# Ordering GpSimd's subtractions, the weight conversions and the activation in the last stage of a fused attention and mixture kernel

## The chip, the cores and the metric
The kernel runs on one core of one Trainium2 chip. The metric is the device time of one execution in microseconds. Before the change it is 782.74 us, the median of three runs (780.12 to 784.16).

## The reference, cut to what matters
The program is attention over 4 x 8 heads with pooled queries, a soft mixture of experts, and a feed-forward block in float32 whose weights come as 64-bit floats. The change touches the last part only:

```python
def _moe2_ref(x, w_in, w_out):          # x 2304 x 512, w_in 512 x 2048, w_out 2048 x 512
    h = x @ w_in
    beta = 1.0
    neg = h <= -beta
    pos = h >= beta
    g = np.where(pos, h, np.where(neg, 0.0, (h + beta) ** 2 / (4.0 * beta)))
    return (g @ w_out).astype(np.float32)
```

x itself is the product c @ slot_out of a 2304 x 32 matrix and a 32 x 512 matrix, so the kernel computes h as c @ (slot_out @ w_in).

## The kernel before, in words
All stages are written out in an order fixed by hand: each engine executes its instructions in the order of the program text, and waits only for data and for buffers. TensorE is first kept busy with attention (to some 450 us after the start), then with the mixture, and from about 535 us on with the last stage.

The last stage works on 36 blocks, SEQ: four quarters q of the 2048 inner columns, and in each nine groups of 256 rows. For block k:

- **h_unit(k)** (L955) lets TensorE multiply Mst (slot_out @ w_in of this quarter) by cT: four matmuls of 256 columns into two PSUM tiles of the pool hp, which has four buffers, so two units. A first clamp or relu goes into the tile cl: on ScalarE where k % 3 is 1 or 2 (L961), on VectorE otherwise (L963).
- **g_unit(k)** (L966) finishes the activation: one or two passes of ScalarE over 1024 columns (L969, L970, L972), then two additions of VectorE, r (L975), which read the PSUM tiles of h. After them the tiles are free for the unit two further on.
- **g_split(k)** (L981) cuts r into two float32r parts: ghi on ScalarE (L984) and glo = r - ghi on GpSimd (L985).
- **o_part(k, tt)** (L1022, matmuls at L1025): 12 output matmuls of 512 columns for each half tt of the rows, ghi by WHI, ghi by WLO, glo by WHI. **o_out** (L1033) adds the PSUM tile to PA in SBUF on VectorE (L1037); in the first quarter it copies, one half on ScalarE (L1041), one on VectorE (L1039). In the last quarter it also issues the store. The pool po of these PSUM tiles has four buffers and is shared with M and its copies.

Beside this the weights are turned from 64-bit to 32-bit floats: **cv_abs** (L185, L189) on ScalarE and the four steps of **cv_step** (L191; L196, L198, L201, L204) on VectorE, the last of which issues the load two pieces on, on SP's queue. Conversion n of 12 to 31 belongs to the block listed in CVB. A converted piece of w_out is split by **w_hi** (ScalarE, L898) and **w_lo** (L902; GpSimd for the quarters 1 to 3, VectorE for quarter 0). **m_mm(q)** (L926) multiplies slot_out by the converted w_in of quarter q and splits the result into Mhl; **m_rep(q)** (L935) spreads it by four matmuls (Mr) into Mst, half on ScalarE (L946), half on VectorE (L944). MB lists the block of m_mm; m_rep follows a block later.

What sets the order around the change is the loop over k: conversion of block k, then ahead(k + 4) (L1051), which runs unit_step(k + 3): g_split(k + 1), g_unit(k + 2), h_unit(k + 3). Then the outputs:

```python
            conv(k, 0, 4)
            ahead(k + AHEAD + 1)
            if sp:
                w_lo(*sp)
            if k < len(SEQ) - 1:
                o_part(k, 0, pos[0])
                ...
                o_out(k, 0, pos[0])
                o_part(k, 1, pos[1])
                o_out(k, 1, pos[1])
                conv_abs(k + 1)
```

Blocks 0 and 1 of the activation go through first_unit (L999) in smaller pieces, and block 0 is mixed by hand with units 2 and 3.

Of the kernel before, what the change touches and what calls it, by code (L numbers as in the profile page):

```python
# [48 lines left out]
def fused_kernel(ctx: ExitStack, tc: tile.TileContext, q, k, v, phi, w1, w2, w_in, w_out, out):  # L49
# [123 lines left out]
    cv = {}  # L173
# [479 lines left out]
    with tc.manual_schedule():  # L653
# [239 lines left out]
            nc.sync.dma_start(out=Wst[:, x:x + 4, :], in_=cv_dr[:, x:x + 4, :])  # L893
        soT = wsp.tile([128, 4, NS], F32, name="soT")
        Mhl = wsp.tile([128, 2, 128], F32R, name="Mhl")

        def w_hi(q, j):
            nc.scalar.activation(out=WHI[q % 2][:, j, :], in_=Wst[:, j, :], func=AF.Copy)  # L898

        def w_lo(q, j):  # L900
            eng = nc.gpsimd if q else nc.vector
            eng.tensor_tensor(out=WLO[q % 2][:, j, :], in0=Wst[:, j, :], in1=WHI[q % 2][:, j, :].bitcast(F32), op=ALU.subtract)  # L902

        for e in range(E_):
            s2o(e, 1)
# [47 lines left out]
            return ps  # L953

        def h_unit(k):  # L955
            cl = t_p.tile([128, 4, TB], F32, tag="cl", name=f"cl{k}")
# [9 lines left out]
        def g_unit(k):  # L966
            cl, ps = hq[k]
            if k % 3:
                nc.scalar.activation(out=cl, in_=cl, func=AF.Relu, scale=-1.0, bias=two)  # L969
                nc.scalar.activation(out=cl, in_=cl, func=AF.Square, scale=-0.5, bias=ones)  # L970
            else:
                nc.scalar.activation(out=cl, in_=cl, func=AF.Square, scale=-0.5, bias=half)  # L972
            r = hq[k] = t_p.tile([128, 4, TB], F32, tag="r", name=f"r{k}")
            for a in (0, 2):
                nc.vector.scalar_tensor_tensor(out=r[:, a:a + 2], in0=ps[a // 2], scalar=-1.0, in1=cl[:, a:a + 2], op0=ALU.max, op1=ALU.add)  # L975

        def g_tiles(k):
# [1 line left out]
            glo[k] = g_p.tile([128, 4, TB], F32R, tag="glo", name=f"glo{k}")  # L979

        def g_split(k):  # L981
            r = hq.pop(k)
# [4 lines left out]
        def unit_step(i):  # L987
            if 3 <= i - 2 < len(SEQ):
                g_split(i - 2)
            if 4 <= i - 1 < len(SEQ):  # L990
                g_unit(i - 1)
            if i < len(SEQ):
                h_unit(i)


        FU = [(0, 0, 1), (0, 1, 2), (0, 2, 3), (0, 3, 4), (1, 0, 2), (1, 2, 4)]
        fu = {}
# [48 lines left out]
        def o_tiles(k):  # L1046
            return [po_tile(f"po{k}_{tt}") for tt in range(2)]

        nu = 4

        def ahead(n):  # L1051
            nonlocal nu
            while nu < min(n, len(SEQ) + 2):
                unit_step(nu)
                nu += 1

        cvb = dict(zip(CVB, range(12, 32)))

        def conv(k, i0, i1):
            if k in cvb:  # L1060
                for i in range(i0, i1):
                    cv_step(cvb[k], i)

        def conv_abs(k):
            if k in cvb:
                cv_abs(cvb[k])

        def split_of(k):
            if k in cvb and cvb[k] % 8 >= 4:
                return cvb[k] // 8, cvb[k] % 8 - 4  # L1070

        c_xpose(1)
        m_mm(0)
# [14 lines left out]
        for k in range(len(SEQ)):  # L1088
            if k:
                pos = o_tiles(k)  # L1090
            if k == 0:
                o_first(0, pos, 0)
                first_unit(5)
                o_first(0, pos, 1)
                first_unit(6)
                h_unit(2)
                g_unit(2)
                o_first(0, pos, 2)
                h_unit(3)
# [5 lines left out]
                conv_abs(1)  # L1105
                continue
            sp = split_of(k - 1)
            if sp:
                w_hi(*sp)
            conv(k, 0, 4)  # L1110
            ahead(k + AHEAD + 1)
            if sp:
                w_lo(*sp)
# [51 lines left out]
```

## Time and profile before

| what | before |
|---|---|
| median of three runs | 782.74 us |
| the profiled execution's own time | 780.04 us |
| its span, first to last instruction | 778.3 us |
[...]
| busy: TensorE, VectorE, ScalarE, GpSimd | 744.0, 618.3, 464.8, 125.1 us |
| instructions | 18103 |

The page shows one profiled execution. [...] The starts of matmuls tell the pace. VectorE is busy in 79% of the span, GpSimd almost only in the last stage. Rows below are named by their group.

### The profile page before, as it was taken

To read this page: it belongs to the slowest core of one execution; us is meant where nothing else is said; L and a number is where in the kernel's file an instruction comes from. 1 tells how busy PE (TensorE), PEld (TensorE's weight loads), DVE (VectorE), ACT (ScalarE), POOL (GpSimd) and SP (SyncE) were. 2 spreads that over 40 slices of the span, in tenths; PEclk is the share of its full clock that TensorE was granted. 3 is DMA by queue.
4 is the path that set the end of the run, shared out by engine and by line. 5 is a ranking of instruction groups with operands and counts; after the bars stand their busy time and mean duration, and the time that the engine had idled before them with its cause. 6 is when DMAs were issued, how large, how long until landed. Compare 5 with 4: busy or idle time off the path is not lost.

```text
span 778.3 us, 18103 instructions
## 1 busy us (share of the span) xinstructions
PE 744.0 (96%) x7422; PEld 544.6 (70%) x7422; DVE 618.3 (79%) x1000; ACT 464.8 (60%) x853; POOL 125.1 (16%) x86
## 2 busy tenths in 40 slices
PE   7789999999999999999999998999899999999998
PEld 6567777766777757777657765436677777778887
DVE  5788898988989969989969774525799998987443
ACT  4246667667567657667656665106876766567660
POOL 7200000000000000000000000002363445246441
PEclk8899999999999999999999999999999999999999
DMA  9697478758667838867938466992112211200122
GB/s 211 125 216 178 92 209 203 158 151 194 159 163 196 210 82 197 194 167 166 238 64 237 141 213 228 365 391 106 52 57 81 83 54 55 82 27 1 55 96 94
DMA packets 133603, 116.55 MB, mean 150 GB/s; under 512 B 80144, under 2 KB 98832, under 8 KB 133136
## 3 DMA queue, kind: packets, MB, share of 16 engines
q1 hardware_dynamic: 133520, 115.40, 54.9%
q8 instruction: 58, 0.95, 0.5%
q14 instruction: 25, 0.20, 0.1%
HBM read 81.85 MB, written 7.86 MB: 115 GB/s over the span
## 4 chain that ended last, share of the span: by engine, by line
PE 71%; DVE 18%; DMA 4%; ACT 3%; issue 3%; SPq 1%; DVEq 0%; ACTq 0%
PE st L366 17%; PE acc L396 16%; PE po L1025 13%; PE mx L300 9%; PE acc L389 3%; DVE r L975 3%; DVE Wst L201 2%; DVE Wst L198 2%; DVE Wst L196 2%; PE tx L434 2%; PE s2o L829 2%; DVE mp L312 2%; PE h L777 1%; DVE pa L1037 1%; PE tb L461 1%
## 5 line engine op out<-in xcount | busy, mean ns | idle before, releaser
L371 ACT ACTIVATE e<-st 128x576 f32<-128x576 f32 x288 | 187.1, 651 | 124.4 <-PE st L366 120.0
L312 DVE TENSOR_REDUCE mp<-mx 128x1 f32<-128x576 f32 x282 | 211.6, 754 | 42.8 <-PE mx L300 42.4
L396 PE MATMUL acc<-e,vf 128*64 128x288 f32 x1152 | 193.8, 408 | 0.0
L300 PE MATMUL mx<-K,q 128*64 128x288 f16 x1152 | 124.6, 297 | 10.6 <-DVE mp L312 3.9
L366 PE MATMUL st<-q,K 128*64 128x288 f16 x1152 | 122.3, 287 | 6.7 <-ACT e L371 4.8
L366 PE MATMUL st<-q,S 128*64 128x288 f16 x1152 | 122.2, 286 | 0.0
L379 DVE TENSOR_TENSOR es<-es,e 128x576 f32<-128x576 f32 x160 | 119.8, 750 | 0.0
L300 PEld LDWEIGHTS <-q 128*64 128x64 f16 x1152 | 66.5, 111 | 70.4 <-issue 24.8
L1025 PE MATMUL po<-whi,ghi 128*128 128x512 f32 x280 | 110.7, 395 | 0.0
L1025 PE MATMUL po<-wlo,ghi 128*128 128x512 f32 x280 | 110.0, 393 | 0.0
L1025 PE MATMUL po<-whi,glo 128*128 128x512 f32 x280 | 109.7, 392 | 0.0
L985 POOL TENSOR_TENSOR glo<-r,ghi 128x1024 fp32r<-128x1024 f32 x34 | 83.0, 2440 | 119.6 <-ACT ghi L984 119.5
L366 PEld LDWEIGHTS <-K 128*64 128x64 f16 x1152 | 68.5, 109 | 24.1 <-issue 14.6
L396 PEld LDWEIGHTS acc<-e,vf 128*64 128x64 f32 x1152 | 78.4, 137 | 5.5 <-ACT e L371 1.6
L754 POOL MEMSET xfer<- 128x1024 f32 x1 | 1.0, 957 | 471.0 <-PE pb L557 471.0
L366 PEld LDWEIGHTS <-S 128*64 128x64 f16 x1152 | 69.9, 110 | 3.0
L1037 DVE TENSOR_TENSOR pa<-po,pa 128x512 f32<-128x512 f32 (+1 forms) x54 | 35.8, 682 | 36.8 <-PE po L1025 36.4
L1025 PEld LDWEIGHTS po<-whi,glo 128*128 128x128 f32 x280 | 53.2, 190 | 11.4
L1025 PEld LDWEIGHTS po<-whi,ghi 128*128 128x128 f32 x280 | 53.5, 191 | 10.8 <-ACT cl L961 0.2
L1025 PEld LDWEIGHTS po<-wlo,ghi 128*128 128x128 f32 x280 | 53.5, 191 | 9.7
L984 ACT ACTIVATE ghi<-r 128x1024 fp32r<-128x1024 f32 x34 | 36.0, 1059 | 36.5 <-DVE r L975 36.5
L975 DVE SCALAR_TENSOR_TENSOR r<-h,cl 128x512 f32<-128x512 f32 x68 | 43.6, 683 | 12.1 <-ACT cl L970 10.6
(197 smaller groups left out, 873.5 us busy)
## 6 DMA issues: line engine op xcount, KB each, us to landing
w<-in_moe_w_dram SPq DMA_DIRECT2D x31, 1024.0 KB, 7.5
vf<-in_v_dram SPq DMA_DIRECT2D x16, 576.0 KB, 4.4
kf<-in_k_dram SPq DMA_DIRECT2D x30, 288.0 KB, 3.6
f<-in_moe_w_in_dram SPq DMA_DIRECT2D x16, 512.0 KB, 4.3
f<-in_moe_w_out_dram SPq DMA_DIRECT2D x16, 512.0 KB, 3.6
qf<-in_q_dram SPq DMA_DIRECT2D x30, 256.0 KB, 4.6
S<-K SPq DMA_DIRECT2D x16, 288.0 KB, 3.2
out_dram<-pa SPq DMA_DIRECT2D x17, 256.0 KB, 2.0
```

The source lines that it names most:

```text
L300: nc.tensor.matmul(ps[p0:p1, i, 0:HQ], lhsT=q1[P][:, t, p0:p1], rhs=kk[:, j * HQ:(j + 1) * HQ], start=True, stop=True)
L312: nc.vector.tensor_reduce(out=mp[P][:, t, a:a + 1], in_=ps[:, :, 0:HQ], op=ALU.max, axis=AX.XY)
L366: nc.tensor.matmul(ps[c0:c0 + 64, i, 0:HQ], lhsT=kk[:, ci, c0:c0 + 64], rhs=f[:, sl[i]], start=first, stop=not first)
L371: nc.scalar.activation(out=e, in_=ps[:, :, 0:HQ], func=AF.Exp, scale=ESC)
L379: nc.vector.tensor_tensor(out=Es[P, n, h][:, i0:i1], in0=a[:, i0:i1], in1=b[:, i0:i1], op=ALU.add)
L389: nc.tensor.matmul(acc[P, i][32 * j:32 * j + 32, HQ:HQ + c1 - c0], lhsT=ones.to_broadcast([128, 32]), rhs=src[:, j % 2, c0:c1], start=Fals ...
L396: nc.tensor.matmul(acc[P, i][h * 64:(h + 1) * 64, 0:HQ], lhsT=vt[P][:, h, c, :], rhs=E[P, c, h][:, i, :], start=(c == 0), stop=(c == NK - ...
L975: nc.vector.scalar_tensor_tensor(out=r[:, a:a + 2], in0=ps[a // 2], scalar=-1.0, in1=cl[:, a:a + 2], op0=ALU.max, op1=ALU.add)
L984: nc.scalar.activation(out=ghi[k], in_=r, func=AF.Copy)
L985: nc.gpsimd.tensor_tensor(out=glo[k], in0=r, in1=ghi[k].bitcast(F32), op=ALU.subtract)
L1025: nc.tensor.matmul(ps, lhsT=a, rhs=b, start=st_, stop=sp)
L1037: nc.vector.tensor_tensor(out=t, in0=po, in1=t, op=ALU.add)
```

## The change
In the last stage, from block 4 on, the order in a block becomes: conversion (or two low parts of w_out), g_unit(k + 3), the absolute value for the next block's conversion, a ScalarE copy of one column out of what the conversion or low part wrote last (junk), and g_split(k + 2). As ScalarE works in order, ghi and with it glo start only when VectorE has finished the conversion. h_unit(k + 4) stands between the two halves of the outputs. Blocks 1 to 3 have steps of their own that bring the activation one block further ahead, with no such copy. Every unit has one half of its first pass on ScalarE and one on VectorE, and 512-wide ScalarE passes. The low parts go to VectorE, two in a block, in blocks without a conversion (5, 6, 15, 16, 25, 26), with their high parts on ScalarE the block before; conversions are in blocks 1 to 4, 7 to 14 and 17 to 24. m_mm is one block later (3, 11, 21), m_rep in the same block after its second half.

```diff
-AHEAD = 3
-CVB = 1, 2, 3, 4, 5, 6, 7, 8, 9, 10, 11, 13, 14, 15, 17, 18, 19, 21, 22, 24
-MB = {1: 2, 2: 10, 3: 20}
+MB = {1: 3, 2: 11, 3: 21}
...
         def w_lo(q, j):
-            eng = nc.gpsimd if q else nc.vector
-            eng.tensor_tensor(out=WLO[q % 2][:, j, :], in0=Wst[:, j, :], in1=WHI[q % 2][:, j, :].bitcast(F32), op=ALU.subtract)
+            nc.vector.tensor_tensor(out=WLO[q % 2][:, j, :], in0=Wst[:, j, :], in1=WHI[q % 2][:, j, :].bitcast(F32), op=ALU.subtract)
...
-            ps = []
-            for a in (0, 2):
-                ps.append(h_mm(k, a, a + 2))
-                if k % 3:
-                    nc.scalar.activation(out=cl[:, a:a + 2], in_=ps[-1], func=AF.Relu, scale=-1.0, bias=ones)
-                else:
-                    nc.vector.tensor_scalar(out=cl[:, a:a + 2], in0=ps[-1], scalar1=-1.0, scalar2=1.0, op0=ALU.max, op1=ALU.min)
+            ps = [h_mm(k, a, a + 2) for a in (0, 2)]
+            nc.scalar.activation(out=cl[:, 0:2], in_=ps[0], func=AF.Relu, scale=-1.0, bias=ones)
+            nc.vector.tensor_scalar(out=cl[:, 2:4], in0=ps[1], scalar1=-1.0, scalar2=1.0, op0=ALU.max, op1=ALU.min)
...
-            if k % 3:
-                nc.scalar.activation(out=cl, in_=cl, func=AF.Relu, scale=-1.0, bias=two)
-                nc.scalar.activation(out=cl, in_=cl, func=AF.Square, scale=-0.5, bias=ones)
-            else:
-                nc.scalar.activation(out=cl, in_=cl, func=AF.Square, scale=-0.5, bias=half)
+            nc.scalar.activation(out=cl[:, 0:2], in_=cl[:, 0:2], func=AF.Relu, scale=-1.0, bias=two)
+            nc.scalar.activation(out=cl[:, 2:4], in_=cl[:, 2:4], func=AF.Square, scale=-0.5, bias=half)
+            nc.scalar.activation(out=cl[:, 0:2], in_=cl[:, 0:2], func=AF.Square, scale=-0.5, bias=ones)
...
-            for a in (0, 2):
+            for a in (2, 0):
                 nc.vector.scalar_tensor_tensor(out=r[:, a:a + 2], ...)
...
                 h_unit(2)
+                o_first(0, pos, 2)
                 g_unit(2)
-                o_first(0, pos, 2)
-                h_unit(3)
+                o_first(0, pos, 3)
                 g_split(2)
-                g_unit(3)
-                o_first(0, pos, 3)
...
+            steps = [(h_unit, 3), (g_unit, 3)], [(h_unit, 4)], [(g_split, 3)]
+            if k == 2:
+                steps = [(g_unit, 4), (g_split, 4)], [(h_unit, 5)], [(g_unit, 5)]
+            elif k == 3:
+                steps = [(g_split, 5), (h_unit, 6), (g_unit, 6)], [(h_unit, 7)], []
+            elif k > 3:
+                steps = [(g_unit, k + 3), (g_split, k + 2)], [(h_unit, k + 4)], []
...
+                if k > 3:
+                    d = aux(k)
+                    g_unit(k + 3)
+                    aux_ahead(k + 1) if AUX.get(k + 1, " ")[0] == "c" else None
+                    if d is not None:
+                        nc.scalar.activation(out=junk, in_=d[:, 0:1], func=AF.Copy)
+                    g_split(k + 2)
+                else:
+                    go(0)
                 o_part(k, 0, pos[0])
+                o_out(k, 0, pos[0])
+                go(1)
                 for q, b in MB.items():
                     if k == b:
                         m_mm(q)
-                    if k == b + 1:
+                if k <= 3:
+                    aux(k)
+                    go(2)
+                    aux_ahead(k + 1) if AUX.get(k + 1, " ")[0] == "c" else None
+                aux_ahead(k + 1) if AUX.get(k + 1, " ")[0] == "s" else None
+                o_part(k, 1, pos[1])
+                for q, b in MB.items():
+                    if k == b:
                         m_rep(q)
-                o_out(k, 0, pos[0])
-                o_part(k, 1, pos[1])
                 o_out(k, 1, pos[1])
-                conv_abs(k + 1)
```

Here aux(k) issues the conversion or the two low parts of block k and returns what was written last; aux_ahead(k + 1) issues the absolute value or the two high parts for the next block.

## Rows read from the trace of the kernel before
**Rows 1.** The page's engine table: busy us (share of the span), instructions.
```profile
PE 744.0 (96%) x7422; PEld 544.6 (70%) x7422; DVE 618.3 (79%) x1000; ACT 464.8 (60%) x853; POOL 125.1 (16%) x86
```
**Rows 2.** Stretches: busy us of each engine, granted clock, DMA share, GB/s.
```profile
core 0: us, PE busy (x) PEld busy (x) DVE busy (x) ACT busy (x) POOL busy (x), PEclk, DMA share, GB/s
...
577.00:585.00 8.00, 7.48 (x27) 5.93 (x28) 7.90 (x9) 6.02 (x8) 4.11 (x2) 0.79 0.21 69
555.00:705.00 150.00, 143.56 (x727) 114.67 (x726) 136.38 (x176) 104.27 (x135) 69.86 (x33) 0.99 0.20 64
```
**Rows 3.** The chain of waits, 680 to 720: start us, us, what.
```profile
682.17 1.01 PE M L930 x32
...
705.16 0.47 PE h L952 x4
705.63 5.47 PE po L1025 x24
```
**Rows 4.** TensorE's timeline: start, us, instruction, [idle before, releaser].
```profile
540.06 0.62 PE L1031 MATMUL po<-whi,ghi 128*128 128x512 f32 x2
...
547.25 1.27 PE L952 MATMUL h<-cT,Mst 128*128 128x256 f32 x4 [2.96 <-DVE r L975]
...
570.37 0.40 PE L1025 MATMUL po<-whi,ghi 128*128 128x512 f32 x1
...
577.43 1.10 PE L952 MATMUL h<-cT,Mst 128*128 128x256 f32 x4 [1.44 <-DVE r L975]
...
578.60 0.50 PE L1025 MATMUL po<-wlo,ghi 128*128 128x512 f32 x1
...
582.24 0.39 PE L1025 MATMUL po<-wlo,ghi 128*128 128x512 f32 x1
...
646.60 1.07 PE L952 MATMUL h<-cT,Mst 128*128 128x256 f32 x4 [0.95 <-DVE r L975]
```
**Rows 5.** Groups by line, 490 to 779, VectorE: busy us, mean ns, idle before.
```profile
L201 DVE SCALAR_TENSOR_TENSOR Wst<-f,Wst 128x512 int32<-128x512 int32 x20 | 24.1, 1206 | 0.7
L196 DVE TENSOR_SCALAR Wst<-Wst 128x512 f32<-128x512 f32 x20 | 22.4, 1119 | 0.0
...
L198 DVE TENSOR_SCALAR Wst<-Wst 128x512 int32<-128x512 int32 x20 | 20.8, 1039 | 0.7
...
L204 DVE SCALAR_TENSOR_TENSOR Wst<-f,Wst 128x512 int32<-128x512 int32 x20 | 15.8, 790 | 0.7
...
L902 DVE TENSOR_TENSOR wlo<-Wst,whi 128x512 fp32r<-128x512 f32 x4 | 3.0, 749 | 0.0
```
**Rows 6.** VectorE's timeline: start us, us, instruction, [idle before, releaser].
```profile
546.50 1.29 DVE L975 SCALAR_TENSOR_TENSOR r<-h,cl 128x512 f32<-128x512 f32 x2 [4.21 <-ACT cl L970]
...
552.08 0.42 DVE L196 TENSOR_SCALAR Wst<-Wst 128x512 f32<-128x512 f32 x1
...
553.72 0.69 DVE L204 SCALAR_TENSOR_TENSOR Wst<-f,Wst 128x512 int32<-128x512 int32 x1
...
571.20 0.77 DVE L944 CAST Mst<-Mr 64x256 fp32r<-64x256 f32 x2
572.00 0.69 DVE L1039 COPY pa<-po 128x512 f32<-128x512 f32 x1
...
600.60 2.78 DVE L201 SCALAR_TENSOR_TENSOR Wst<-f,Wst 128x512 int32<-128x512 int32 x1
```
**Rows 7.** GpSimd's timeline, 598 to 612.
```profile
600.40 2.43 POOL L985 TENSOR_TENSOR glo<-r,ghi 128x1024 fp32r<-128x1024 f32 x1 [4.63 <-ACT ghi L984]
```
**Rows 8.** ScalarE's timeline.
```profile
542.86 1.25 ACT L961 ACTIVATE cl<-h,cols 128x512 f32<-128x512 f32 x2
...
545.32 1.15 ACT L970 ACTIVATE cl<-cl,cols 128x1024 f32<-128x1024 f32 x1
...
599.26 1.06 ACT L984 ACTIVATE ghi<-r 128x1024 fp32r<-128x1024 f32 x1 [2.73 <-DVE r L975]
...
604.08 0.67 ACT L189 ACTIVATE Wst<-f 128x512 f32<-128x512 f32 x1
```
**Rows 9.** Groups by line, ScalarE, whole span: a one-column activation.
```profile
L516 ACT ACTIVATE cols<-cols 32x1 f32<-32x1 f32 x3 | 0.8, 278 | 0.0
```

More of the change, by code (lines that the diff above doesn't have):

```diff
@@ L895, in fused_kernel @@
         Mhl = wsp.tile([128, 2, 128], F32R, name="Mhl")
+        junk = wsp.tile([128, 1], F32, name="junk")
         def w_hi(q, j):
@@ L955, in h_unit @@
         def h_unit(k):
+            if k >= len(SEQ):
+                return
             cl = t_p.tile([128, 4, TB], F32, tag="cl", name=f"cl{k}")
-            ps = []
-            for a in (0, 2):
-                ps.append(h_mm(k, a, a + 2))
-                if k % 3:
-                    nc.scalar.activation(out=cl[:, a:a + 2], in_=ps[-1], func=AF.Relu, scale=-1.0, bias=ones)
-                else:
-                    nc.vector.tensor_scalar(out=cl[:, a:a + 2], in0=ps[-1], scalar1=-1.0, scalar2=1.0, op0=ALU.max, op1=ALU.min)
+            ps = [h_mm(k, a, a + 2) for a in (0, 2)]
+            nc.scalar.activation(out=cl[:, 0:2], in_=ps[0], func=AF.Relu, scale=-1.0, bias=ones)
+            nc.vector.tensor_scalar(out=cl[:, 2:4], in0=ps[1], scalar1=-1.0, scalar2=1.0, op0=ALU.max, op1=ALU.min)
             hq[k] = cl, ps
         def g_unit(k):
+            if k >= len(SEQ):
+                return
             cl, ps = hq[k]
-            if k % 3:
-                nc.scalar.activation(out=cl, in_=cl, func=AF.Relu, scale=-1.0, bias=two)
-                nc.scalar.activation(out=cl, in_=cl, func=AF.Square, scale=-0.5, bias=ones)
-            else:
-                nc.scalar.activation(out=cl, in_=cl, func=AF.Square, scale=-0.5, bias=half)
+            nc.scalar.activation(out=cl[:, 0:2], in_=cl[:, 0:2], func=AF.Relu, scale=-1.0, bias=two)
+            nc.scalar.activation(out=cl[:, 2:4], in_=cl[:, 2:4], func=AF.Square, scale=-0.5, bias=half)
+            nc.scalar.activation(out=cl[:, 0:2], in_=cl[:, 0:2], func=AF.Square, scale=-0.5, bias=ones)
             r = hq[k] = t_p.tile([128, 4, TB], F32, tag="r", name=f"r{k}")
-            for a in (0, 2):
+            for a in (2, 0):
                 nc.vector.scalar_tensor_tensor(out=r[:, a:a + 2], in0=ps[a // 2], scalar=-1.0, in1=cl[:, a:a + 2], op0=ALU.max, op1=ALU.add)
@@ L981, in g_split @@
         def g_split(k):
+            if k >= len(SEQ):
+                return
             r = hq.pop(k)
@@ L1047, in o_tiles, with aux, aux_ahead @@
             return [po_tile(f"po{k}_{tt}") for tt in range(2)]
[L1049 to L1070, printed above, removed]
+        AUX = [("c", n) for n in range(12, 16)] + [("s", 1), ("s", 1)]
+        for q in (2, 3):
+            AUX += [("c", n) for n in range(8 * q, 8 * q + 8)] + [("s", q), ("s", q)]
+        AUX = {k + 1: x for k, x in enumerate(AUX)}
+        def aux(k):
+            kind, n = AUX.get(k, (None, 0))
+            if kind == "c":
+                for i in range(4):
+                    cv_step(n, i)
+                return cv[n][1]
+            if kind == "s":
+                j = 0 if AUX.get(k + 1) == AUX[k] else 2
+                for i in range(j, j + 2):
+                    w_lo(n, i)
+                return WLO[n % 2][:, j + 1, :].bitcast(F32)
+        def aux_ahead(k):
+            kind, n = AUX.get(k, (None, 0))
+            if kind == "c":
+                cv_abs(n)
+            if kind == "s":
+                j = 0 if AUX.get(k + 1) == AUX[k] else 2
+                for i in range(j, j + 2):
+                    w_hi(n, i)
         c_xpose(1)
@@ L1096, in fused_kernel, with go @@
                 h_unit(2)
+                o_first(0, pos, 2)
                 g_unit(2)
-                o_first(0, pos, 2)
-                h_unit(3)
+                o_first(0, pos, 3)
                 g_split(2)
-                g_unit(3)
-                o_first(0, pos, 3)
                 for tt in range(2):
                     o_out(0, tt, pos[tt])
-                conv_abs(1)
+                aux_ahead(1)
                 continue
[L1107 to L1113, printed above, removed]
-            if k < len(SEQ) - 1:
+            steps = [(h_unit, 3), (g_unit, 3)], [(h_unit, 4)], [(g_split, 3)]
[5 more added lines that the diff above has]
+                steps = [(g_unit, k + 3), (g_split, k + 2)], [(h_unit, k + 4)], []
+            def go(i):
+                for f, x in steps[i]:
+                    f(x)
+            if k < len(SEQ) - 1:
+                if k > 3:
[7 more added lines that the diff above has]
+                    go(0)
                 o_part(k, 0, pos[0])
+                o_out(k, 0, pos[0])
+                go(1)
                 for q, b in MB.items():
```

7 lines of the change are left out of this document (removed).

## The prediction
> **What bounds the kernel now.** I read the page's engine table first: TensorE is busy 96% of the span [rows 1], which invites the reading that nothing can be won. That busy time counts waits between matmuls and half-clock matmuls, so I went on to the chain of waits at the end of the last stage. There a block without any wait is one group of four h matmuls, 0.47 us, and 24 output matmuls, 5.47 us: 5.94 us a block, 0.228 us an output matmul [rows 3]. These are the units of the whole sum. TensorE's timeline gives the real pace [rows 3, 4]: from the first output matmul of block 4 (570.37) to that of block 24 (705.63) are 20 blocks in 135.3 us. Their own work is 20 x 5.94 = 118.8, and two rounds of M (1.01) and its copies Mr (taken like an h group, 0.47) make 3.0 more, so 121.8. **13.5 us are lost there.** Another 2.96 us were lost in one wait before block 1.
>
> The waits in TensorE's timeline name VectorE's r as releaser (2.96, 1.44, 0.95) [rows 4], and over 555 to 705 VectorE is busy 136.4 of 150 us [rows 2]: it sets the pace there, not TensorE. Why is it slow? The groups by line show the four steps of a w-conversion [rows 5]: 22.4 + 20.8 + 24.1 + 15.8 = 83.1 us for 20 conversions, 4.16 each, while one that met nothing ran from 552.08 to 554.41, 2.33 us [rows 6]. So 83.1 - 20 x 2.33 = 36.5 us are waiting inside VectorE's instructions. The reader sees whom they wait for in one pair: the step that began at 600.60 took 2.78 us [rows 6], and GpSimd's subtraction ran from 600.40 to 602.83 [rows 7]. The two queue for one another. r itself, from PSUM, keeps 1.29 for two [rows 6].
>
> After a long wait TensorE also runs at half clock: granted 0.79 over 577 to 585 [rows 2]. Nine matmul starts from 578.60 to 582.24 took 3.64 us in place of 9 x 0.228 = 2.05: 1.6 us [rows 4]. That followed the wait of 1.44; after the 0.95 I see none.
>
> **The change, part by part.**
>
> *From block 4 on: the tie, and activation a block further ahead.* Per block VectorE then has a conversion 2.33, r 1.29, one clamp (half of every unit, where a third of the units had two; taken like one r, 0.65) and two additions of at most 0.69: about 5.6 us, under 5.94 [rows 3, 6]. The 12 low parts that leave GpSimd cost VectorE 0.75 at most, two in a block without a conversion [rows 5]: 1.5 in place of 2.33, so nothing. ScalarE gets 512-wide passes in place of 1024-wide: 0.62 each where the wide one took 1.15 [rows 8]: with four of them, 1.06 for ghi, 0.67 for the absolute value and the tie it has some 4.5 of 5.94 us, hidden under TensorE. What is queued behind the tie on ScalarE is ghi, the relu of the next unit and the w_hi copies. ghi(k+2) is needed two blocks later, and h(k+4) needs only r(k+2), done the block before; one full block of lead, 5.9 us, covers the wait. SP gets the same loads at the same places, the conversions' last steps; outputs leave from block 27, after them. So TensorE should run free at 5.94.
>
> [...] The rows give 2 x 0.62 - 1.15 = 0.1 us. [...] I keep the rows' 0.1.
>
> *M's copies move into M's own block.* m_rep now follows the second half, and the block's last addition is queued on VectorE behind the two Mst casts. The next block's PSUM buffer is the one that this addition frees. So TensorE waits, after Mr (0.47), for Mr's end (about 0.4), casts 0.77, addition 0.69 (the copy at 572.00 is of its size) [rows 6] and a hop of 0.1: 1.96 - 0.47 = 1.5 us, three times. The trace has no such wait; bounds are 0 (the addition is let past) and 2.96, the longest wait seen [rows 4]. I take 1.5.
>
> *The start, blocks 0 to 3.* Here nothing is tied, and the new order is walked through by queue:
> - h of unit 3 leaves block 0, so its last parts run on from 540.06 [rows 4], and with h (0.47) and half a block (2.73) TensorE is at h of unit 4 by 546.0. ScalarE starts unit 2 at 542.86 as before; four 512 passes (0.6) end at 545.3, r ends 546.2. The wait of 2.96 becomes 0.3, and its half clock goes. TensorE ends block 2 at 555.4.
> - But ScalarE then does ghi(2) (1.06), a copy and an absolute value (0.6 each, as 604.08 has 0.67 [rows 8]) and unit 3's four passes: 551.0. r of unit 3 ends 551.8, clamp 552.4. Conversion 12 then meets glo(3), whose ghi starts at 552.2 and which arrives at 553.3: 2.1 + 2.3. Then a copy (0.6) and r of unit 4 (1.3): 558.8. h of unit 6, first in block 3, needs that r: **a wait of 3.4 us**.
> - Conversion 13 meets glo(4) likewise: clamp 0.6, 4.5, r 1.3, so h of unit 7 comes at 565.0 where TensorE was ready at 562.1: **3 us**.
> - M, the second half, then Mr waits 1.2 for Mhl behind r(6); conversion 14 (2.2), casts and addition put block 4's first output matmul at **574.1**, after a last wait of 3.0 (its 1.5 for M's copies is in it). Before it was 570.37 [rows 4]: 3.7 later.
>
> Half clocks between these waits only fill the next wait; the one after the last costs 1.5.
>
> **The sum.** Lost from block 4 on before: 13.5. After: two M waits 2 x 1.5, the half clock behind the start's last wait 1.5, and one more behind one of the two M waits, 1.5, since 1.44 brought one and 0.95 none. 13.5 - 6.0 = 7.5; less the later start, 3.7: **3.8 us less**. The profiled execution took 780.04 (span 778.3), so 776.2; it stood 2.7 under the median 782.74, so on that scale **778.9**, 0.49% faster. A measurement of this kernel can tell about 0.5% (3.9 us) from no change, so the likeliest case lies right at that edge.
>
> **Rivals.**
> 1. *The start is lighter.* In blocks 1 and 2 the conversions are through before glo arrives, or GpSimd is the one that waits. Each is then 2.1 shorter and block 4 starts 4.2 us earlier: 774.7; with the clock unbroken after it, 773.2. For it: the walk is good to half a microsecond per block only, and glo(3) arrives 1.4 us before conversion 12 would have ended. Against it: in the trace it was VectorE that waited, 36.5 us of it.
> 2. *The M waits and the clock eat the rest.* Both M waits bring a half clock (1.5 more), and hops in the start add 0.5 to 1: a gain of 1.3 to 1.8, so 781. For it: 1.44 did it. Against: 0.95 did not.
> 3. *The tie becomes the pace (slower).* In blocks 4, 7 to 14 and 17 to 24 one ring must close in a block: conversion 2.33, tie, ghi 1.06, glo 2.43, next conversion [rows 6 to 8]. The tie, 128x1, is bounded by nothing and by the 0.28 of a 32x1 activation [rows 9]; with hops of 0.1 the ring is 5.9 to 6.2, against 5.94. At 6.2 the excess, 17 x 0.26 = 4.4, stays under the lead of 5.9 us. From 17x - 5.9 = 3.8, a ring of 6.51, nothing is won. If the absolute value ahead of the tie waits for its load, and the ring takes the 6.76 that blocks 4 to 23 took before (135.3 / 20), 17 x 0.82 - 5.9 = 8.0 is lost against 3.8 won: 786.9. Against it: the load is issued a block ahead of its use. [...]
> That the change does not do what it says belongs here: if glo runs into the next conversion, the wait is moved, not removed.
>
> **How the numbers follow.** Forecast (gain 2.3 to 5.3) 0.50, about half of it over 3.9; rival 1 0.22; rival 2 0.17; rival 3 0.11. Faster: 0.26 + 0.22 = 0.48. Same: 0.24 + 0.17 = 0.41. Slower: 0.11. The range, 773.5 to 784.5, takes in rival 1, rival 2, and M waits anywhere from 0 to 2.96; it leaves out rival 3's upper part and the ends. The forecast's own range is 777.4 to 780.4.
>
> **What would show it.** Right: conversions of 2.3 us from block 4 on; h groups without a wait from block 4; waits of about 3 us before h of units 6 and 7 and before block 4, 1.5 after each Mr; block 4's first output matmul near 574. Wrong: conversions still near 4.16, glo's start still inside them, a block pace over 6.0, or waits of ScalarE's tie on anything but the conversion.

## The result, and the profile after

The changed kernel takes 771.03 us, the median of four runs (769.61 to 774.1), against 782.77 for the kernel before in the same comparison: ratio 0.986, interval 0.982 to 0.990. That is 11.7 us faster, below the whole forecast range. The profiled execution took 770.55 (span 768.8). In it the last stage begins 1.6 us later (ScalarE's first relu of unit 2 at 544.42, before 542.86 [rows 8]), so I count from that relu: its last full block starts 210.1 us after it, before 221.1. **11.0 us of the gain arise behind that relu, in the last stage.**

The page's engine table, to be held against [rows 1]:

```profile
PE 741.1 (96%) x7422; PEld 543.9 (71%) x7422; DVE 604.1 (79%) x1024; ACT 460.4 (60%) x909; POOL 107.1 (14%) x74
```

The shares of TensorE and VectorE have not moved by a point. As before, they tell nothing; the stretches do [rows 2]:

```profile
core 0: us, PE busy (x) PEld busy (x) DVE busy (x) ACT busy (x) POOL busy (x), PEclk, DMA share, GB/s
555.00:565.00 10.00, 7.33 (x26) 5.39 (x24) 9.86 (x11) 6.52 (x11) 4.40 (x2) 0.83 0.17 52
...
575.00:705.00 130.00, 130.00 (x665) 107.64 (x664) 112.56 (x187) 95.77 (x165) 50.63 (x21) 1.00 0.20 65
```

Over 575 to 705 TensorE is busy throughout, at full clock (granted 1.00), and VectorE has 17 us of 130 to spare. VectorE's groups by line over 490 to 779 show why [rows 5]:

```profile
L198 DVE SCALAR_TENSOR_TENSOR Wst<-f,Wst 128x512 int32<-128x512 int32 x20 | 18.1, 904 | 0.7
L201 DVE SCALAR_TENSOR_TENSOR Wst<-f,Wst 128x512 int32<-128x512 int32 x20 | 13.8, 692 | 0.7
L899 DVE TENSOR_TENSOR wlo<-Wst,whi 128x512 fp32r<-128x512 f32 x16 | 13.2, 856 | 0.5 <-ACT whi L896 0.4
L193 DVE TENSOR_SCALAR Wst<-Wst 128x512 f32<-128x512 f32 x20 | 11.5, 577 | 0.0
L195 DVE TENSOR_SCALAR Wst<-Wst 128x512 int32<-128x512 int32 x20 | 8.6, 428 | 0.7
```

The four steps of 20 conversions take 52.0 us, 2.60 each, where they took 4.16. TensorE's timeline (start, us, instruction, [idle before, releaser]) answers to [rows 4]:

```profile
559.60 1.30 PE L949 MATMUL h<-cT,Mst 128*128 128x256 f32 x4 [2.30 <-DVE r L970]
560.70 0.63 PE L1013 MATMUL po<-whi,ghi 128*128 128x512 f32 x1
...
562.84 0.40 PE L1013 MATMUL po<-whi,glo 128*128 128x512 f32 x1
...
565.73 1.01 PE L949 MATMUL h<-cT,Mst 128*128 128x256 f32 x4 [1.09 <-DVE r L970]
...
571.51 0.74 PE L937 MATMUL Mr<-Mhl,Sel 128*128 128x256 f32 x4 [0.78 <-DVE Mhl L930]
572.10 0.40 PE L1013 MATMUL po<-whi,ghi 128*128 128x512 f32 x1
...
621.49 0.64 PE L937 MATMUL Mr<-Mhl,Sel 128*128 128x256 f32 x4
621.97 0.39 PE L1013 MATMUL po<-whi,ghi 128*128 128x512 f32 x1
```

Three waits are left, all in the start: before h of units 6 and 7 and before Mr. After 571.51 there is none. Behind the first, five output matmuls take 0.43 each (560.70 to 562.84) in place of 0.233, at half clock (granted 0.53 over 560 to 563), and that costs 1.0 us. The last stage's chain of waits (start, us, what) shows blocks of two lengths [rows 3]:

```profile
587.67 5.59 PE po L1013 x24
...
624.86 0.47 PE h L949 x4
625.34 5.46 PE po L1013 x24
```

24 output matmuls take 5.59 us in quarters 0 and 2 and 5.46 in 1 and 3. Before, they took 5.47 in quarter 2 as well [rows 3]. That is a loss which I had not foreseen.

### The profile page after: what moved, and what is told of

Read it like the earlier page. It is cut to its first block, busy times and chain, and to the rows that moved or that the text cites. A ratio compares the mean times of both kernels' runs of the same rounds, so it can differ in the third digit from the quotient of the medians.

```text
span 768.8 us, 18141 instructions
## 1 busy us (share of the span) xinstructions
PE 741.1 (96%) x7422; PEld 543.9 (71%) x7422; DVE 604.1 (79%) x1024; ACT 460.4 (60%) x909; POOL 107.1 (14%) x74
## 4 chain that ended last, share of the span: by engine, by line
PE 83%; DVE 8%; ACT 3%; DMA 3%; issue 1%; SPq 1%; DVEq 0%; ACTq 0%
PE po L1013 23%; PE st L363 17%; PE acc L393 16%; PE mx L297 9%; PE acc L386 3%; DVE mp L309 2%; PE h L774 2%; PE tx L431 2%; PE s2o L826 2%; PE h L949 2%; PE tb L458 1%; DVE es L376 1%; DMA f<-in_moe_w_in_dram 1%; DMA qf<-in_q_dram 1%; PE tr L420 1%
## 5 line engine op out<-in xcount | busy, mean ns | idle before, releaser
L447 ACT ACTIVATE xnr<-tx,ss 96x64 f32<-96x64 f32 x180 | 40.9, 306 | 7.0 <-PE tx L431 6.8
```

The lines of the kernel that those rows point to most:

```text
L447: nc.scalar.activation(out=xn[:, 3 * i + t3, c0:c0 + D], in_=ps[0:TT, i, t3 * 128 + h * D:t3 * 128 + (h + 1) * D], func=AF.Copy, scale=ss[ ...
```

## The experiments

For each kernel the table has, besides time and ratio, the mean of a conversion (four groups by line, as above), the start (first relu of unit 2 to block 4's first output matmul) and the stretch from there to block 27's. 140.1 is the stretch without a wait at 5.94 us a block, as e5 and e11 show it. A mean hides two kinds of conversion: one that meets no subtraction takes 2.23 us of busy time, one that meets one fully takes 4.3 or more. Each kernel was timed beside the kernel before, which took 782.77 us beside the change and 779.9 to 780.7 beside the others; so times of different rows are best compared by ratio. Start and stretch are of one profiled execution each.

| kernel | us | ratio (interval) | conversion | start | blocks 4 to 27 |
|---|---|---|---|---|---|
| before | 782.77 | | 4.16 | 27.5 | 153.0 |
| after | 771.03 | 0.986 (0.982 to 0.990) | 2.60 | 27.7 | 141.8 |
| e1 no tie | 770.56 | 0.987 (0.985 to 0.989) | 3.00 | 27.7 | 142.7 |
| e2 buffers moved by 64 bytes | 769.32 | 0.986 (0.984 to 0.987) | 2.62 | 27.7 | 141.6 |
| e3 before, buffers moved | 779.78 | 1.000 (0.999 to 1.002) | 4.15 | 27.5 | 153.1 |
| e4 tie in the start too | 768.08 | 0.985 (0.983 to 0.987) | 2.39 | 26.4 | 141.8 |
| e5 no new tile | 768.84 | 0.984 (0.982 to 0.987) | 2.73 | 27.7 | 140.1 |
| e16 no tie, no new tile | 767.90 | 0.984 (0.982 to 0.986) | 2.91 | 27.7 | 140.2 |
| e11 = e4 + e5 | 765.22 | 0.982 (0.981 to 0.983) | 2.52 | 26.4 | 140.1 |
| e6 no tie, low parts on GpSimd | 772.56 | 0.989 (0.987 to 0.991) | 3.00 | 27.7 | 143.7 |
| e7 h first | 770.04 | 0.986 (0.983 to 0.988) | 2.56 | 28.1 | 142.3 |
| e13 no tie, h first | 775.24 | 0.994 (0.992 to 0.996) | 2.99 | 28.2 | 146.0 |
| e10 no tie, clamps in thirds | 770.41 | 0.987 (0.985 to 0.989) | 2.90 | 28.4 | 141.9 |
| e14 no tie, ghi first | 786.72 | 1.009 (1.007 to 1.011) | 4.00 | 27.7 | 158.9 |
| e8 before, h mid-block | 779.46 | 0.999 (0.997 to 1.000) | 4.18 | 22.5 | 156.9 |
| e9 before, low parts on VectorE | 775.65 | 0.995 (0.993 to 0.996) | 3.69 | 26.5 | 149.0 |
| e12 before, passes ahead of ghi | 784.04 | 1.004 (1.002 to 1.006) | 3.91 | 26.4 | 157.0 |
| e15 e12 + halved clamps | 780.03 | 1.000 (0.998 to 1.001) | 3.92 | 24.3 | 155.0 |
| e17 e12 + e9 | 783.41 | 1.004 (1.002 to 1.006) | 3.91 | 26.5 | 157.4 |
| e18 e17 + a block further ahead | 784.62 | 1.006 (1.004 to 1.009) | 3.78 | 30.1 | 155.4 |

### Is it the tie?

e1 takes the tie out (the tile stays and is filled once on GpSimd); e16 takes out the tile too.

```diff
-                    if d is not None:
-                        nc.scalar.activation(out=junk, in_=d[:, 0:1], func=AF.Copy)
```

> The changed kernel without the tie: the one-column copy ahead of ghi is gone (its tile stays, written once, so that all addresses stay). Theory 1, the tie brings the gain: the subtractions meet the conversions again, a conversion goes from 2.6 us back to about 4, VectorE needs about 7 us a block, and the time is 4 to 8 us above the changed kernel's 771.0. Theory 2, the lead brings it (h stands between the halves, a half block later against r): the conversions lengthen, but TensorE's h groups still don't wait, and the time is within 1 us of 771.0.

> The changed kernel without tie and without any new tile, so no buffer moves. Theory A (the tie is worth 1 us from block 4 on, as the run without it said, and the address 2): 768.0 to 769.5, ratio 0.985. Theory B (with the shorter pace the conversions meet the subtractions more often and the tie is worth more): 770 or above, ratio 0.987 or more.

**The tie is worth nothing that can be measured here** (ratios 0.986 and 0.987, and 0.984 for both e5 and e16). Without it conversions lengthen by 0.40 us (2.60 to 3.00), 8 us in all, and the stretch by 0.8. The mean hides that in e1 of the 18 conversions after the first two, five meet a subtraction fully (4.3 to 4.5 us) and twelve meet none (2.23). Why most stay free is in e1's timelines of ScalarE, GpSimd and VectorE:

```profile
599.99 0.67 ACT L186 ACTIVATE Wst<-f 128x512 f32<-128x512 f32 x1 [0.80 <-DMA f<-in_moe_w_in_dram]
600.57 1.05 ACT L982 ACTIVATE ghi<-r 128x1024 fp32r<-128x1024 f32 x1
```

```profile
601.69 2.61 POOL L983 TENSOR_TENSOR glo<-r,ghi 128x1024 fp32r<-128x1024 f32 x1 [3.07 <-ACT ghi L982]
```

```profile
601.34 0.69 DVE L201 SCALAR_TENSOR_TENSOR Wst<-f,Wst 128x512 int32<-128x512 int32 x1
601.95 1.28 DVE L971 SCALAR_TENSOR_TENSOR r<-h,cl 128x512 f32<-128x512 f32 x2
603.14 0.68 DVE L1026 TENSOR_TENSOR pa<-po,pa 128x512 f32<-128x512 f32 x1
```

With no tie, ghi still comes only at 600.57, because on ScalarE the next unit's passes and an absolute value stand ahead of it, and the absolute value here waits 0.80 us for its load; so glo starts as the conversion ends. From there it runs beside r and the addition, each of which reads one operand from PSUM, and delays neither (1.28, 0.68).

In the start, where nothing is tied, it is otherwise. In the profile after, VectorE's and GpSimd's timelines:

```profile
554.69 2.84 DVE L198 SCALAR_TENSOR_TENSOR Wst<-f,Wst 128x512 int32<-128x512 int32 x1
```

```profile
554.57 2.41 POOL L982 TENSOR_TENSOR glo<-r,ghi 128x1024 fp32r<-128x1024 f32 x1 [3.19 <-PE h L949]
```

e4 moves g_split(3) and g_split(4) behind conversions 12 and 13 and ties them:

```diff
-                steps = [(g_unit, 4), (g_split, 4)], [(h_unit, 5)], [(g_unit, 5)]
+                steps = [(g_unit, 4)], [(h_unit, 5)], [(g_split, 4)]
...
-                    aux(k)
+                    d = aux(k)
+                    if k == 2:
+                        g_unit(5)
+                    if k < 3:
+                        nc.scalar.activation(out=junk, in_=d[:, 0:1], func=AF.Copy)
```

> The changed kernel with the same tie in blocks 1 and 2 too: g_split(3) behind conversion 12, and g_split(4) behind conversion 13 and g_unit(5). If the waits of 2.3 and 1.1 us before h of units 6 and 7 come from the conversions being held up by the subtractions (2.84 and 2.77 us in their third step), these steps go to 0.7, the half clock goes, and the time falls by 2 to 3.5 us, to 768. Rival: the tied glo(3) comes too late for block 3 instead, the wait moves from h to the output matmuls, and the time stays within 1 us of 771.

The step of 2.84 falls to 0.69, and the start by 1.3 us (27.7 to 26.4); in the ratio (0.985 against 0.986) that is not clear of the noise. The wait before h of unit 7 goes, but the one before h of unit 6 grows to 2.70, and its half clock stays (six output matmuls at 0.43 each, 557.69 to 560.25). The tie has put another wait in the collision's place: on ScalarE unit 4's passes now stand behind it, and VectorE's r waits for them (ScalarE's and VectorE's timelines of e4):

```profile
552.73 0.20 ACT L1129 ACTIVATE junk<-Wst 128x1 f32<-128x1 f32 x1 [2.60 <-DVE Wst L201]
```

```profile
555.75 1.29 DVE L970 SCALAR_TENSOR_TENSOR r<-h,cl 128x512 f32<-128x512 f32 x2 [2.46 <-ACT cl L966]
```

### The pace of 5.59

The new tile is allocated ahead of whi1, pa, ghi, glo, r and others, and behind whi0 and cT. In the built program I read that it moves the former by 32 bytes; no trace holds addresses. e3 adds only the tile, filled once, to the kernel before; e2 makes the tile 64 bytes wide in place of 4; e5 writes the tie into a column that is there already:

```diff
e3, to the kernel before
+        junk = wsp.tile([128, 1], F32, name="junk")
+        nc.gpsimd.memset(junk, 0.0)
e2
-        junk = wsp.tile([128, 1], F32, name="junk")
+        junk = wsp.tile([128, 16], F32, name="junk")[:, 0:1]
e5
-        junk = wsp.tile([128, 1], F32, name="junk")
+        junk = cols[0:128, 12:13]
```

> The kernel before with nothing but the 4-byte tile added (written once), so that the same tiles move by 32 bytes. Theory A: its output matmuls of quarters 0 and 2 go from 0.228 to 0.233 us, and since it waits for VectorE in many of these blocks, 0.5 to 2.2 us are added: 783.3 to 785. Rival, activity: starts and time stay (782.8).

> The changed kernel with the tie's tile 64 bytes wide instead of 4, so that the tiles allocated behind it move by 64 bytes and not by 32. Theory A, addresses: the output matmuls of the quarters 0 and 2 start every 0.228 us instead of 0.233, 18 blocks x 24 x 0.005 = 2.2 us, and the time is about 768.8. Rival, activity: the slower starts come from what the other engines do in those blocks, the starts stay at 0.233 and the time at 771.0.

> The changed kernel, but the tie writes an unused column of a tile that is there already, so nothing behind it moves in SBUF. Theory A (the 32 bytes by which the new tile moves the buffers behind it cost TensorE 0.005 us per output matmul): the matmuls start every 0.228 us in all four quarters, as in the kernel before, and the time is 1.5 to 2.5 us under the changed kernel's 771.0, at ratio 0.983 or below. Theory B (the pace belongs to the new order of work, by which the engines reach SBUF at other moments): 0.233 stays in quarters 0 and 2, and the ratio stays at 0.985 to 0.987.

e3's chain of waits, last block of quarter 2 and a block of quarter 3:

```profile
717.03 5.59 PE po L1027 x24
...
729.05 5.47 PE po L1027 x24
```

With nothing changed but the tile, the kernel before takes on the two paces, so they come from where the buffers lie and not from the order of work. A tile of 64 bytes cures nothing (e2: 0.233 us a matmul in quarters 0 and 2). In the kernel before the slower pace costs no time (ratio 1.000), which fits that VectorE sets the pace there. In the changed kernel it costs 1.7 us of the stretch (141.8 to 140.1 in e5), 2.5 from e1 to e16; the ratios alone (0.986 and 0.984, 0.987 and 0.984) don't separate them. The slow quarters 0 and 2 are those whose matmuls read whi0, which stays, beside ghi and glo, which move; quarters 1 and 3 read whi1, which moves with them. That points at the distance between two operands, but no run moves one buffer alone, so which two meet badly is open.

### ScalarE's order

e14 is e1 with ghi ahead of the passes again:

```diff
                     d = aux(k)
+                    g_split(k + 2)
                     g_unit(k + 3)
...
-                    g_split(k + 2)
```

> The changed kernel without the tie, and from block 4 on ScalarE's ghi(k+2) stands ahead of unit k+3's passes and the absolute value, as it stood ahead of them in the kernel before. To be compared with the run without the tie (770.56, ratio 0.987, conversions 3.0 us each). Theory A (it is ScalarE's new order that keeps GpSimd's subtraction behind the conversion even without a tie: ghi comes 2.8 us later in ScalarE's queue): ghi starts at the end of r again, the subtraction runs into the next conversion, conversions go to 3.7 us or more, waits for r come back and the time is 4 us or more above 770.6. Theory B (VectorE's load and the earlier h are the gain): conversions may grow, but no wait comes back from block 4 on and the time stays within 1.5 us of 770.6.

**This one edit loses 16.2 us against e1.** e14's timelines of ScalarE, GpSimd, VectorE and TensorE:

```profile
594.81 1.06 ACT L982 ACTIVATE ghi<-r 128x1024 fp32r<-128x1024 f32 x1 [2.22 <-DVE r L971]
```

```profile
595.95 2.57 POOL L983 TENSOR_TENSOR glo<-r,ghi 128x1024 fp32r<-128x1024 f32 x1 [4.17 <-ACT ghi L982]
```

```profile
596.28 2.52 DVE L195 TENSOR_SCALAR Wst<-Wst 128x512 int32<-128x512 int32 x1
```

```profile
623.74 0.73 PE L938 MATMUL Mr<-Mhl,Sel 128*128 128x256 f32 x4 [3.96 <-DVE Mhl L931]
...
694.48 1.22 PE L938 MATMUL Mr<-Mhl,Sel 128*128 128x256 f32 x4 [3.91 <-DVE Mhl L931]
```

ghi now starts as soon as r ends, glo falls into the next conversion, and a conversion takes 4.0 us on the mean, near the 4.16 before the change. VectorE then falls behind, and Mr waits 4 us twice for what is queued on it.

Is the order enough by itself? e12 swaps two steps in unit_step of the kernel before. e15 adds the halved clamps of the changed kernel, e17 (to e12) the low parts on VectorE, e18 (to e17) the lead.

```diff
e12
-            if 3 <= i - 2 < len(SEQ):
-                g_split(i - 2)
             if 4 <= i - 1 < len(SEQ):
                 g_unit(i - 1)
+            if 3 <= i - 2 < len(SEQ):
+                g_split(i - 2)
e18
-AHEAD = 3
+AHEAD = 4
```

> The kernel before with one edit: in each step of the activation the passes of unit k+2 stand ahead of ghi(k+1) on ScalarE. Theory A (the order of ScalarE is enough by itself): conversions fall from 4.16 to about 3 us, the waits for r go, and the time falls by 6 us or more, to 774 or below. Theory B (in the kernel before the passes of two units in three wait for nothing on VectorE, so they are through before r and ghi still starts where r ends; only a clamp on VectorE behind r makes them late): the subtraction keeps running into the next conversion, conversions stay above 3.6 us, and the time is within 3 us of before.

> The kernel before with the passes ahead of ghi on ScalarE and with one half of every unit's clamp on VectorE. Theory A (order alone): no better than the kernel with the order alone, within 1.5 us of it. Theory B (order and clamp behind r together): conversions at 3.2 us or less and 4 us or more under the kernel with the order alone, so 774 or below. Where both are wrong, the two blocks of activation that the changed kernel keeps between ghi and its output are needed as well, and conversions stay above 3.6 us in both kernels.

> The kernel before with two edits: the passes ahead of ghi on ScalarE, and the low parts of w_out on VectorE at their old places. Alone, the first gave nothing (ratio 1.004, conversions 3.9 us) and the second 4.3 us (ratio 0.9945, 3.7 us). Theory A (both together keep GpSimd out of the conversions): conversions at 3.2 us or less and the time at 773 or below, ratio under 0.991. Theory B (the subtraction still has to be ready within one block, and gets its start from r): conversions stay above 3.5 us and the time within 2 us of the low parts alone, 773.7 to 777.7.

> As the run with order and low parts, and every step of the activation one block further ahead (the constant AHEAD 4 instead of 3; the h matmuls stay ahead of the first half). Theory A (order and low parts are enough): from block 4 on no better than that run, within 1.5 us. Theory B (lead is the third part that is needed): conversions fall under 3.2 us and the time is 3 us or more below that run, unless the start loses it: block 1 now has the steps of two blocks.

None is faster than before; conversions stay at 3.8 to 3.9 us. e17 fell outside both its theories: with the new order the low parts on VectorE lose the gain that they bring alone (783.41 against e9's 775.65). And in this kernel the halved clamps are worth 4 us on top of the order (e15 against e12, 1.000 against 1.004, intervals apart), though they do not shorten the conversions. e12's timelines of VectorE and GpSimd:

```profile
609.35 2.78 DVE L204 SCALAR_TENSOR_TENSOR Wst<-f,Wst 128x512 int32<-128x512 int32 x1
```

```profile
609.18 2.40 POOL L985 TENSOR_TENSOR glo<-r,ghi 128x1024 fp32r<-128x1024 f32 x1 [2.81 <-ACT ghi L984]
```

The collision moved: of e12's steps the fourth is held up most (1.69 us on the mean, where a free one takes 0.69). So in the changed kernel without the tie the order is needed, but it does not carry the gain alone; what it must be joined with is not settled. Not tried in the kernel before: the blocks that the change leaves free of conversions, and h between the halves together with this order.

### Lead and load

e7 puts h_unit(k + 4) ahead of the first half, e13 does so without the tie; e8 puts h_unit(k + 3) between the halves in the kernel before.

```diff
e7, e13
+                if k > 3:
+                    go(1)
                 o_part(k, 0, pos[0])
                 o_out(k, 0, pos[0])
-                go(1)
+                if k <= 3:
+                    go(1)
e8, and h_unit(i) out of unit_step
                 o_part(k, 0, pos[0])
+                if k + 3 < len(SEQ):
+                    h_unit(k + 3)
```

> The changed kernel, but from block 4 on the h matmuls of unit k+4 stand ahead of the block's first half again instead of between its halves: half a block, 2.7 us, less time for r. Theory A (the gain is the lead of the activation: more time between r and the h that needs its buffers): waits of TensorE for r appear in blocks 7 to 24 and the time is 3 us or more above 771. Theory B (VectorE's load is under TensorE's 5.94 us a block, so any lead will do): no wait from block 4 on and the time stays within 1 us of 771.

> The changed kernel without the tie, with the h matmuls of unit k+4 ahead of the first half of block k from block 4 on. With the tie this place of h cost nothing (ratio 0.986). Theory A (h between the halves makes ScalarE's relu wait to the middle of a block, and that sets the phase of ghi, so that tie and middle place can stand in for each other): without both, conversions go to 3.7 us or more and the time is 4 us or more above 770.6. Theory B (either is dispensable by itself): conversions stay at 3.0 to 3.3 us and the time within 1.5 us of 770.6.

> The kernel before with one edit: the h matmuls of unit k+3 stand between the two halves of block k's outputs instead of ahead of them. Theory A (before, the lead was too short: r was late by a wait of 1 to 3 us at a time, while VectorE had time enough on the mean): the waits before h in blocks 4 to 24 go for the most part and the time falls by 6 us or more, to 774 or below. Theory B (VectorE is full, 136 of 150 us, so a later h only moves the wait): the time falls by 0 to 2.7 us, half a block once.

With the tie, h's place is worth nothing (e7). Without the tie, the early h costs 4.7 us against e1 (e13), as theory A said of the time. But conversions stay at 3.0 us, against its reason. As I read it, the collisions are no longer than in e1, they only meet an h that leaves r half a block less. The largest part is one wait before h, of 2.06 us, just ahead of block 5's output matmuls, in TensorE's timeline of e13:

```profile
577.98 1.11 PE L950 MATMUL h<-cT,Mst 128*128 128x256 f32 x4 [2.06 <-DVE r L971]
578.92 0.40 PE L1014 MATMUL po<-whi,ghi 128*128 128x512 f32 x1
```

**So tie and place of h stand in for each other**, which e1 and e7 alone could not show. In e8 the start is 5.0 us shorter and the rest 3.9 longer, and TensorE's and VectorE's timelines show an output matmul that waits for a PSUM buffer:

```profile
626.70 0.80 PE L1022 MATMUL po<-whi,ghi 128*128 128x512 f32 x1 [3.93 <-DVE Mst L944]
```

```profile
626.22 0.77 DVE L944 CAST Mst<-Mr 64x256 fp32r<-64x256 f32 x2
627.02 1.29 DVE L1034 TENSOR_TENSOR pa<-po,pa 128x512 f32<-128x512 f32 x2
```

It is near the wait that I had forecast for the change, but not the same: the matmul starts behind the first cast of Mr and ahead of the additions, so what it waits for is Mr's buffer, behind a conversion in VectorE's queue, and not the buffer that an addition frees.

e6 gives the low parts of quarters 1 to 3 back to GpSimd, without the tie; e9 takes them off it in the kernel before; e10 has the clamps and passes of the kernel before, without the tie.

```diff
e6 (e9 is the reverse)
-            nc.vector.tensor_tensor(out=WLO[q % 2][:, j, :], ...
+            eng = nc.gpsimd if q else nc.vector
+            eng.tensor_tensor(out=WLO[q % 2][:, j, :], ...
e10, and g_unit in the same way
+                if k % 3:
+                    nc.scalar.activation(out=cl[:, a:a + 2], in_=ps[-1], ...
+                else:
+                    nc.vector.tensor_scalar(out=cl[:, a:a + 2], in0=ps[-1], ...
```

> The changed kernel without the tie and with the low parts of the quarters 1 to 3 on GpSimd again, at their new places. To be compared with the run without the tie (770.56, ratio 0.987). Theory A (the gain comes from the load taken off VectorE's conversions): twelve subtractions of about 1.2 us on GpSimd stand where VectorE has no conversion in its block, so the conversions stay near 3.0 us and the time stays within 1 us of 770.6: then the moved low parts are not the gain. Theory B (GpSimd's low parts were what pushed the subtractions of the activation into the conversions): conversions go to 3.5 us or more, waits before h groups come back in the quarters 1 and 2, and the time is 3 to 8 us above 770.6.

> The kernel before with one edit: the low parts of w_out of the quarters 1 to 3 are subtracted on VectorE instead of GpSimd, at their old places (one in each of 12 blocks that have a conversion). Theory A (GpSimd's 17.5 us in 12 subtractions are a third of what the conversions wait for): 12 x 1.46 us of waiting go and 12 x 0.75 come, so VectorE's full stretches shorten by up to 8 us and the time falls by 4 to 8, to 772 to 776. Theory B (those blocks have no wait worth having, or the subtractions of the activation fall into the conversions all the same): VectorE gets 9 us more, and the time stays within 2 us of before.

> The changed kernel without the tie, with the clamps in thirds as in the kernel before: both halves on ScalarE for two units in three, both on VectorE for the third, passes of 1024 columns. To be compared with the run without the tie (770.56, conversions 3.0 us). Theory A (the order of ScalarE is enough): conversions stay at 3.0 to 3.3 us and the time within 1.5 us of 770.6. Theory B (the clamp on VectorE behind r is what makes the passes, and ghi behind them, late): in two units of three ghi starts where r ends, conversions go to 3.6 us or more and the time is 4 us or more above 770.6.

Before the change the low parts on GpSimd cost 4.3 us (e9). In the changed kernel, where their blocks have no conversion, e6 stands 2.0 us above e1 (0.989 against 0.987, intervals that overlap), and conversions stay at 3.0. In the profiles the stretch is 1.0 longer: block 5 takes 1.8 us more, with a wait of 1.21 before h and a slow h group behind it (0.94 from 581.24 to the first output matmul, in place of 0.47; the granted clock was 1.00), and a wait of 0.56 before Mr that e1 has is gone. The halved clamps are worth nothing in the changed kernel (e10).

### Both edits that helped together

> The changed kernel with both edits that helped by themselves: the tie also in blocks 1 and 2, and the tie's result in a column that is there already, so that no buffer moves. Theory A (the two gains are separate, 1.3 us in the start and 2.2 in the pace): 3.5 us under the changed kernel, 767.5 or below, ratio 0.981 to 0.983. Theory B (they are one and the same, since the start's length depends on the pace): ratio 0.984 to 0.985, as for either alone.

e11 takes 765.22 us, ratio 0.982, the lowest of all. Its interval lies under those of e1 and e2 and overlaps with those of after, e4, e5 and e16. In the profile the two gains add up: start 26.4, stretch 140.1.

## Why the prediction was wrong, point by point

**From block 4 on TensorE runs free at 5.94: right**, but for the pitch, a term that the sum lacked (1.7 us). Behind the start no h waits, and a conversion takes 2.2 to 2.9 us of busy time, 2.4 on the mean.

**The tie: mechanism right, cause wrong.** GpSimd out of the conversions is what pays (e14, e9). But I put it all on the tie, and without it ScalarE's new order, with h between the halves, does the same work (e1, e16, e14, e13). I had walked through that order in the start, where I counted everything ahead of ghi, and not from block 4 on, where I took ghi to start when it could. (A free conversion has 2.23 us of busy time, 2.33 from start to end; so of the 83.1 us busy before, 38.5 were waiting and not 36.5.)

**A price per pass of 0.1: small, and between two readings.** The passes after start 0.62 apart (596.15, 596.78, 597.40 in ScalarE's timeline below). Of e12's two passes of 1024 columns the second, which reads what the first wrote, starts 1.18 behind it; the ghi of another unit starts 1.06 behind the second:

```profile
600.45 1.15 ACT L969 ACTIVATE cl<-cl,cols 128x1024 f32<-128x1024 f32 x1
601.63 1.15 ACT L970 ACTIVATE cl<-cl,cols 128x1024 f32<-128x1024 f32 x1
602.69 1.04 ACT L984 ACTIVATE ghi<-r 128x1024 fp32r<-128x1024 f32 x1
```

So a split costs 2 x 0.62 - 1.18 = 0.06 where a pass waits for the one before it, and 2 x 0.62 - 1.06 = 0.18 where it does not. Plain copies pay less than that: in the profile after two whi of 512 columns start 0.52 apart, and a ghi of 1024 is followed after 0.95, so 2 x 0.52 - 0.95 = 0.09. TensorE set the pace behind the start, so none of this moved the time there.

**M's copies move into M's own block: this step failed.** It said that the next block's PSUM buffer is the one that the last addition frees. The trace after shows block 4's first output matmul at 572.10, straight behind Mr, while that addition (the copy of block 3's second half) ran later on VectorE:

```profile
573.74 0.77 DVE L941 CAST Mst<-Mr 64x256 fp32r<-64x256 f32 x2
574.54 0.69 DVE L1027 COPY pa<-po 128x512 f32<-128x512 f32 x1
```

So block 4's tile lies in another buffer, free by then, and TensorE waits for none of it; at 621.97 too it goes on without a wait. I had counted the four buffers off in turn instead of asking which were free. What hung on it: 3.0 us in the start's last wait, 2 x 1.5 of waits, 2 x 1.5 of half clocks behind them, 9.0 together. My lower bound for the wait was 0, and I took 1.5 with no row of such a wait. In e8, with another order, an output matmul does wait for a buffer of M's copies (3.93), but not for an addition's. Nor did the length of a wait tell in these runs whether a half clock follows, as I had priced it: 1.44 brought one in the kernel before (granted 0.79 [rows 2]), 2.06 brought none in e13 (granted 1.00).

**The start: collisions right, sum wrong.** Conversions 12 and 13 took 4.5 and 4.4 us from first start to last end, against 4.4 and 4.5 forecast. But taking these collisions away shortens the start by 1.3 only (e4), and the waits were 2.30, 1.09 and 0.78 against 3.4, 3.0 and 1.2; the last one, of 3.0, did not come. Counted from the relu, block 4 began 0.2 us later than before, not 3.7.

**The sum.** Forecast from the relu on: 3.8 less. Add 9.0 for the failed step and 0.5 for the rest of the start, take off 1.7 for the pitch and 0.5 for the two rounds of M, priced too low (e11's free blocks 4 to 27 take 140.1, by my units 23 x 5.94 + 3.0 = 139.6): 11.1. Take off 0.2 more for a misreading: 705.63 is where the chain puts the output matmuls of block 24, and in TensorE's timeline the first starts at 705.47. That makes 10.9. Measured: 11.0.

**Rivals.** Rival 1, the lighter start, had the direction for a reason that did not hold: the collisions of the start were there, and its times kept the M waits. Rival 2 added half clocks behind the same waits, which did not come. Rival 3's ring does close within TensorE's block, with little to spare (5.87 from tie to tie, 593.91 to 599.78, in a block of 6.07). ScalarE's and GpSimd's timelines of after:

```profile
593.91 0.20 ACT L1114 ACTIVATE junk<-Wst 128x1 f32<-128x1 f32 x1 [1.11 <-DVE Wst L201]
594.02 1.04 ACT L981 ACTIVATE ghi<-r 128x1024 fp32r<-128x1024 f32 x1
...
596.15 0.72 ACT L965 ACTIVATE cl<-cl,cols 128x512 f32<-128x512 f32 x1
596.78 0.71 ACT L966 ACTIVATE cl<-cl,cols 128x512 f32<-128x512 f32 x1
597.40 0.71 ACT L967 ACTIVATE cl<-cl,cols 128x512 f32<-128x512 f32 x1
...
599.78 0.20 ACT L1114 ACTIVATE junk<-Wst 128x1 f32<-128x1 f32 x1 [0.88 <-DVE Wst L201]
```

```profile
595.14 2.41 POOL L982 TENSOR_TENSOR glo<-r,ghi 128x1024 fp32r<-128x1024 f32 x1 [3.46 <-DVE r L970]
```

The tie takes 0.20, inside my bounds; glo ends at 597.55, and the next conversion's first step, at 597.19, takes 0.65 where a free one takes 0.42. So that step ended 0.29 after the subtraction beside it, and the other collisions shown look alike: 0.28 (e14), 0.55 (the 2.84 above, and e12).

The range ended at 773.5, above even rival 1's 773.2, because no case had the M waits and their half clocks gone together, though the bounds that I gave allowed it.

## What to carry to other kernels

Before a wait for a buffer goes into a sum, find which buffer the next tile gets and who frees it; where no row shows such a wait, "no wait" is a case of its own, with a chance and with all that hangs on it. Where two engines collide, look at the order on the third engine, the one that feeds them: here it decided in the changed kernel without the tie (e14), though not by itself (e12), and a tie may find such an order fixed already. Take each edit out alone and with its neighbour: tie and place of h look worthless singly and are worth 4.7 us as a pair.

## What the runs showed of the hardware

A tile of four bytes a partition, allocated ahead of other buffers, changed the pitch of float32 matmuls of 512 columns from 0.228 to 0.233 us in two quarters of four (24 in 5.59 us in place of 5.47; e3, where nothing else changed). A tile of 64 bytes in its place kept that (e2, 0.233); no new tile removed it (e5, e16, 0.228). The granted clock was 1.00 at either pitch. GpSimd's subtraction of 1024 columns held up VectorE's steps between SBUF operands by up to 2.2 us (after: 2.84 where a free one takes 0.69), but not the instructions with one operand in PSUM (e1: r 1.28 for two beside it, as in after without it).
